# Block-causal attention then a gated two-layer network on one core: a planned kernel gets other planned load times, and a few of its operations move to other engines and places

## The chip, the cores and the metric

The program runs on one core of one Trainium2 chip. Its time is the device time of the whole program in microseconds (us), lower is better. The engines are named as the profile names them: PE (TensorE matmuls), PEld (its weight loads), DVE (VectorE), ACT (ScalarE), POOL (GpSimd) and SP (SyncE, which only issues transfers here). ACT and POOL issue transfers as well.

## The reference

Attention over 8 batches of 8 heads, 576 positions of 64 elements, masked by blocks of 64 positions; then two matrix products with an activation between them, over 4608 rows (8 batches x 576 positions) of 512 elements.

```python
scores = (1 / np.sqrt(64)) * q @ k.transpose(0, 1, 3, 2)
scores = np.where(pos[:, None] // 64 >= pos[None, :] // 64, scores, -1e9)
attn = softmax(scores); attn_out = attn @ v
x = attn_out.transpose(0, 2, 1, 3).reshape(4608, 512)
h = x @ w_in                       # 512 -> 2048
g = h * (1.0 / (1.0 + np.exp(-beta * h)))
out = g @ w_out                    # 2048 -> 512
```

q, k, v, w_in and w_out come as float32 and the result is float32. Inside, the kernel multiplies in bf16 and f16.

## The kernel before

The kernel writes no order of its own. It makes a list of operations (`P.op`), each with an engine, a planned duration, the operations that it depends on, the buffers that it takes and a priority `prio` (lower goes first). `Plan.schedule` plays them through in a model of the core and so fixes, once, the order in which each engine issues its instructions; `assign` then gives the semaphore waits. On the chip each engine goes through its own list in that order and waits where it must. For a transfer the plan takes `xfer` (ns) as the time that it holds its queue, and adds a fixed landing time. A changed `xfer` or `prio` therefore changes nothing but the order in which instructions stand on all the engines, as far as the plan runs differently.

**Attention** goes by units of two heads, a *pair*; batch 0 has pairs 0 to 3 (`u` = 0 to 3), batch 1 pairs 4 to 7. In batches 0 and 1 q and k of a pair come as two 256 KB loads (`ST`, L724, buffers ST0 to ST7 by turn, semaphores `s_d_S0_0` to `s_d_S7_0`: q of pair 0 is S0, k of pair 0 is S1, and so on; pair 4 takes S0 and S1 again). Each is cast to bf16 (L731, `QKn`; on POOL except for q of pairs 0 and 3, which DVE casts), turned by PE in four small matmuls (L742), and copied from PSUM to `QKT` by DVE (L752). The scores of a pair are three groups of matmuls in batch 0 (L837), each group with an exponential on ACT (L857, 128x1024 twice and 128x512) into `E`, and a mask: a memset of zeros over the forbidden corner (L865 and L867). `E` is multiplied by V (L912 in batch 0, L1051 later), then divided by the row sums on DVE (L930, L937; later L1063, L1070), turned again (L946) and copied into `xT` (L953), the input of the network. Pair 3's `E` lies in the buffer gT1. The last 64 rows of batch 0 are done apart, "late" (L975 to L1038), from loads of their own (semaphore `s_d_TR0_0`, cast at L692). V of batch 0 comes as 128 KB loads (`s_d_V0_0` to `s_d_V0_7`) and is cast by POOL to `Vn` (L575); V of batch 1 comes as four blocks and two tails (L598, L601) and is cast at L624. From batch 2 on, q and k come in 576 KB loads (L765), POOL casts them (L776) and a transposing transfer on SP turns them (L783).

**The network** goes by chunks of 512 rows, r = 0 to 8. A chunk has 16 FF1 blocks, j = 0 to 15: four 128x512 matmuls of `xT` by a column block of `w_in` (L1297), a tanh on ACT (L1307) and a product on DVE that writes `gT` (L1311). Block j needs part j // 4 of `w_in`. Chunk 0 then does FF2 plainly: 64 matmuls of 128x512 by `w_out` (L1333), sixteen of them for each of four parts of `w_out`. Later chunks use a scheme with fewer products (L1214) on sums that DVE makes (L1158, L1178). The four parts of `w_in` (L524, semaphores `s_d_win0` to 3) and of `w_out` (L529) are cast during their transfer and so are issued by POOL, between its casts. Where PE would stand idle early on, the plan puts fill matmuls on zeros (L548, L457).

What issues a part of the weights is set at the end: `WH()` names, for the four parts of `w_in`, the load whose landing they wait for, and

```python
        for w, o in zip(win, WH()):
            w.deps.append(o)
        for i, w in enumerate(wout):
            w.deps += ld["V", 1, 0] if i < 2 else [ld["K", 8]]
```

so that parts 1, 2 and 3 of `w_in` wait for k of pairs 4, 5 and 5, and parts 0 and 1 of `w_out` for all six loads of V of batch 1.

Of the kernel before, what the change touches and what calls it, by code (L numbers as in the profile page):

```python
# [359 lines left out]
def bass_blockwise_causal_attn__then__act_swish_beta_kernel(  # L360
# [10 lines left out]
    with es:  # L371
# [59 lines left out]
        P = Plan()  # L431
# [53 lines left out]
        for i in range(NQ):  # L485
# [5 lines left out]
            o = P.op("POOL", 120, mk(lambda g, i=i: g.memset(Vn[i][:, 4, :, 64:66], 0.0)), prio=-5)  # L491
# [6 lines left out]
        for i in range(NQ, NE + 1):  # L498
# [10 lines left out]
                  xfer=100, dma=("d_beta", 1), prio=3.45)  # L509
# [3 lines left out]
                  deps=[bt, c2], tiles=[tb], lat=400, mode="full", prio=9)  # L513
# [6 lines left out]
        win, wout = [], []  # L520
# [39 lines left out]
        load, ld, early = {}, {}, []  # L560
        VC = -38.5
        tl = {}
        for b in range(B):
# [27 lines left out]
            for h0, h1, e, tt in PARTS[b]:  # L591

                vs = []
                for i in tt:
# [10 lines left out]
                    if e == "SP":  # L605
                        o = P.op("SP", 300 + 550 * n, fv, tiles=[ts], xfer=1400 * n,
                                 prio=3.5 + 0.1 * (h0 > 0) if b == 0 else 4 * b + (3.5 if b < 2 else 0.5),
                                 dma=["d_V", h0, 1])
                    else:
                        o = P.op("POOL", 150 + 1450 * n, fv, tiles=[t], xfer=1400 * n, prio=-30 if b == 0 else 4 * b + (3.5 if b < 2 else 0.5), dma=["d_VP", h0, 1])  # L610
                        o.after = lastv if b else None
# [36 lines left out]
        def WH():  # L648
            return ld["V", 0, 1], ld["K", 4], ld["K", 5], ld["K", 5]

        xt, spare = [], []
        HALF, LP, VP = (3,), .2, 200 + 2
        copied, more0 = [], []
        early6, rows = [], []
        QKI, QKX = 550, 2700
        for u in range(NU):
            b, c = divmod(u, NPAIR)
# [9 lines left out]
            if b < QB:  # L667

                if c == 0:
# [10 lines left out]
                    for w, src in enumerate((q, k)):  # L680
# [4 lines left out]

                        o = P.op("SP", 650, fl, tiles=[te_], xfer=900, prio=u + 0.5 if b else 3.8, dma=["d_TR", 0, 1])
                        o.pkt = 48.0
# [31 lines left out]
                for w, (nm, src) in enumerate((("Q", q), ("K", k))):  # L719
# [6 lines left out]

                    o = ld[nm, u] = P.op("SP", 540, fl, tiles=[ts], xfer=(760, 950)[b], prio=u, dma=["d_S", 0, 1])
                    o.pkt = 48.0
# [122 lines left out]
            for g0 in range(4 if b else 3):  # L851
                o, ps = qk[g0]
                if g0 < 3:
# [9 lines left out]
                    def fz(g, e, g0=g0, te=te, two=two, off3=off3):  # L863
# [3 lines left out]
                        return g.memset(bass.AP(a.tensor, a.offset, [a.ap[0], [512, 2], [off3, 2], [1, 64]]), 0.0)  # L867
                    zs.append(P.op("DVE" if b or g0 == 2 else "POOL", 160 if g0 != two else 220, fz, deps=[x], tiles=[te], prio=-20 if b or g0 == 2 else -37))
                else:
# [252 lines left out]
        for i, w in enumerate(wout):  # L1122
            w.deps += ld["V", 1, 0] if i < 2 else [ld["K", 8]]

# [302 lines left out]
```

## Time and profile before

| | us |
|---|---|
| time, median of 3 runs | 330.4 (327.89 to 335.31) |
| the profiled execution's time | 329.3 |
| its span, first to last instruction | 327.5 |
| PE busy | 316.4 (97% of the span) |
| DVE busy | 219.9 (67%) |
| ACT busy | 211.8 (65%) |
| POOL busy | 84.5 (26%) |
| mean granted TensorE clock | 0.999 |

The time is 1.8 us longer than the span in the profiled execution: that is what lies around the instructions. Busy time of PE is a union of the matmuls' recorded stretches. Matmuls overlap (one of 128x512 is recorded with 379 ns, while eight of them in a row take 1.73 us), so short waits between them do not show as idle time.

### The profile page before, as it was taken

The page shows a single profiled execution, that of the slowest core. Times are in us where ns is not written, and L with a number is a line of the kernel's source. Part 1 is how long each engine was busy: PE and PEld are TensorE (multiplying, and loading weights), DVE is VectorE, ACT ScalarE, POOL GpSimd, SP SyncE. Part 2 cuts the span into 40 slices and gives each one's busy share as a digit, 9 for nine tenths or more (in the row PEclk, how much of TensorE's full clock was granted, in tenths as well). Part 3 has the DMA queues.
Part 4 walks back from the last instruction along what each step waited for, and adds up shares of the span by engine and source line. Part 5 has one row for each costly group of instructions (what it writes and reads, how often), then busy time and mean ns, then how long its engine had stood idle before and what let it go on. Part 6 is the DMA issues. An engine that isn't in the chain of part 4 may idle for free.

```text
span 327.5 us, 7435 instructions
## 1 busy us (share of the span) xinstructions
PE 316.4 (97%) x3101; PEld 200.3 (61%) x3012; DVE 219.9 (67%) x455; ACT 211.8 (65%) x312; POOL 84.5 (26%) x137
## 2 busy tenths in 40 slices
PE   7698999999999999999999999999999999999996
PEld 2454446445786457854776467666666766666695
DVE  5657857578763789368843996659576866666742
ACT  2769891388557886499657866885978454544521
POOL 4768090073073046103520541150000000000000
PEclk9999999999999999999999999999999999999999
DMA  7999999999999999997999999999030310111023
GB/s 224 225 302 233 215 211 199 169 292 189 226 252 221 222 193 218 186 240 152 196 190 241 231 197 195 199 169 152 0 74 2 104 34 32 62 36 35 6 92 128
DMA packets 156706, 53.58 MB, mean 164 GB/s; under 512 B 139120, under 2 KB 156160, under 8 KB 156672
## 3 DMA queue, kind: packets, MB, share of 16 engines
q1 hardware_dynamic: 144112, 40.46, 65.8%
q10 hardware_dynamic: 8336, 8.46, 8.2%
q0 software_dynamic: 4224, 4.19, 7.8%
q8 instruction: 24, 0.39, 0.5%
q14 instruction: 10, 0.08, 0.1%
HBM read 36.71 MB, written 9.44 MB: 141 GB/s over the span
## 4 chain that ended last, share of the span: by engine, by line
PE 83%; DMA 5%; DVE 4%; ACT 4%; issue 2%; SPq 1%; POOL 1%; POOLq 0%
PE PS L1297 34%; PE PS L1214 29%; PE PS L1051 8%; PE PS L837 6%; PE PS L1333 4%; DMA w_in<-in_moe_w_in_dram 3%; ACT E L857 2%; DMA ST<-in_q_dram 2%; DVE gT L1311 1%; ACT th L1307 1%; DVE QKT L752 1%; SPq L724 1%; DMA xT<-xq 1%; PE PS L1099 1%; PE PS L912 0%
## 5 line engine op out<-in xcount | busy, mean ns | idle before, releaser
L1297 PE MATMUL PS<-xT,w_in 128*128 128x512 bf16 x576 | 137.7, 379 | 3.1 <-DMA w_in<-in_moe_w_in_dram 1.2
L1307 ACT ACTIVATE th<-PS,beta 128x512 f32<-128x512 f32 x144 | 97.0, 701 | 54.9 <-PE PS L1297 53.9
L1311 DVE SCALAR_TENSOR_TENSOR gT<-th,PS 128x512 f16<-128x512 f32 x144 | 95.2, 681 | 35.8 <-ACT th L1307 35.4
L857 ACT ACTIVATE E<-PS 128x1024 bf16<-128x1024 f32 (+1 forms) x90 | 87.5, 1014 | 22.4 <-PE PS L837 21.5
L1297 PEld LDWEIGHTS PS<-xT,w_in 128*128 128x128 bf16 x576 | 53.1, 98 | 58.5 <-issue 2.2
L1214 PE MATMUL PS<-w_out,gT 128*128 128x256 f16 x512 | 63.0, 273 | 0.1
L1214 PEld LDWEIGHTS PS<-w_out,gT 128*128 128x128 f16 x512 | 49.0, 98 | 12.1 <-issue 0.8
L776 POOL CAST QKn<-ST 128x640 bf16<-128x640 f32 x48 | 37.0, 771 | 24.9 <-DMA ST<-in_k_dram 13.9
L624 POOL CAST Vn<-Vs 128x640 bf16<-128x640 f32 x24 | 19.6, 815 | 91.7 <-DMA Vs<-in_v_dram 90.6
L1236 ACT ACTIVATE ost<-PS 128x512 f32<-128x512 f32 x32 | 19.3, 604 | 28.5 <-PE PS L1214 28.5
L1214 PE MATMUL PS<-OV 128*128 128x256 f16 (+1 forms) x264 | 31.8, 270 | 0.0
L1051 PEld LDWEIGHTS PS<-Vn,E 128*128 128x128 bf16 x810 | 27.5, 97 | 3.9 <-issue 0.4
L837 PE MATMUL PS<-QKT 64*128 64x448 bf16 (+7 forms) x292 | 28.6, 295 | 0.5 <-ACT E L857 0.5
L1051 PE MATMUL PS<-Vn,E 128*128 128x65 bf16 x810 | 28.4, 193 | 0.0
L1214 PEld LDWEIGHTS PS<-OV 128*128 128x128 f16 x264 | 24.5, 98 | 6.1 <-issue 0.6
L1178 DVE TENSOR_TENSOR OV<-gT 128x1024 f16<-128x1024 f16 x32 | 23.9, 753 | 0.6
L837 PEld LDWEIGHTS PS<-QKT 64*128 64x128 bf16 (+1 forms) x292 | 13.3, 94 | 17.7 <-issue 3.6
L1070 DVE TENSOR_TENSOR xq<-PS,inv 128x640 bf16<-128x640 f32 x28 | 23.0, 820 | 0.5
L1239 DVE SCALAR_TENSOR_TENSOR ost<-PS,ost 128x512 f32<-128x512 f32 x22 | 15.2, 689 | 9.5 <-PE PS L1214 6.9
L865 DVE MEMSET E<- 64x64 uint32 x57 | 6.3, 112 | 17.9 <-ACT E L857 16.0
L1214 PE MATMUL PS<-OV,gT 128*128 128x256 f16 (+1 forms) x136 | 16.0, 266 | 0.0
L1333 PE MATMUL PS<-w_out,gT 128*128 128x512 f16 x64 | 15.3, 379 | 0.0
(106 smaller groups left out, 189.9 us busy)
## 6 DMA issues: line engine op xcount, KB each, us to landing
out_dram<-ost ACTq DMA_DIRECT2D x32, 256.0 KB, 3.9
ST<-in_q_dram SPq DMA_DIRECT2D x12, 576.0 KB, 6.2
ST<-in_k_dram SPq DMA_DIRECT2D x12, 576.0 KB, 7.2
Vs<-in_v_dram SPq DMA_DIRECT2D x24, 256.0 KB, 4.6
ST<-in_q_dram SPq DMA_DIRECT2D x8, 256.0 KB, 5.9
ST<-in_k_dram SPq DMA_DIRECT2D x8, 256.0 KB, 6.1
w_in<-in_moe_w_in_dram POOLq DMA_DIRECT2D x4, 512.0 KB, 8.4
w_out<-in_moe_w_out_dram POOLq DMA_DIRECT2D x4, 512.0 KB, 8.9
```

The lines of the kernel that those rows point to most:

```text
L624: return g.tensor_copy(Vn[t.slot][:, 0:n, g0:g1, 0:64], Vs[ts.slot][:, 0:n, g0:g1, :])
L776: return g.tensor_copy(QKn[tn.slot][:].rearrange("p a w n -> p (a w n)")[:, 640 * (2 * a + w):][:, 0:640] .rearrange("p (t h d) -> p t h d ...
L837: z = g.matmul(o, QKT[tqk.slot][r, uu % 2, 1, k0:k0 + m], x)
L857: return g.activation(E3[es_(te)][:, g0, :, 0:n], PS[:, ps.slot:ps.slot + 2, 0:n], ACT.Exp, scale=0.125)
L1051: z = g.matmul(o, eblk(te, t, i, h), Vn[Tv.slot][:, t, 2 * c + h, 0:65], start=(t == 0), stop=(t == i))
L1070: return g.tensor_tensor(xq[xq_(tx)][:].rearrange("p i (h d) -> p h i d", h=2), both(pv, 0, 64), x, ALU.mult)
L1178: return P.op("DVE", dve_t(SZ * HC / 2), mk(lambda g: g.tensor_tensor(fo(), fx(), fy(), op)), deps=deps, tiles=tiles, prio=prio)
L1214: x = g.matmul(PS[:, pw.slot, HM * w + c0:HM * w + c1], fa()[:, j, 128 * w:128 * w + 128], fb()[:, j, c0:c1], start=first and (pair or w = ...
L1297: z = g.matmul(PS[:, ph.slot, :], w_in[:, c, 128 * j:128 * j + 128], xT[:, c, row % RX:row % RX + RC], start=(c == 0), stop=(c == 3))
L1307: return g.activation(th[tt.slot][:], PS[:, ph.slot, :], ACT.Tanh, scale=beta[:, j:j + 1])
L1311: return g.scalar_tensor_tensor(out=gT[tg.slot][:, j, :], in0=th[tt.slot][:], scalar=1.0, in1=PS[:, ph.slot, :], op0=ALU.add, op1=ALU.mult)
L1333: z = g.matmul(PS[:, po.slot, 0:d1 - d0], gT[tg.slot][:, j, 128 * w:128 * w + 128], w_out[:, j, d0:d1], start=(j == 0), stop=(j == NJ - 1))
```

## The change

Five edits:

1. The loads of q and k of pairs 0 to 3 get planned queue times of their own, `EARLYX`, instead of 760 ns each; those of batch 0's late rows get 1100 ns instead of 900.
2. The masks of pair 3 are made by DVE instead of POOL (the condition `u == 3`).
3. Part 1 of `w_in` waits for the loads of the late rows (`ld["T", 0]`) instead of k of pair 4; part 2 for k of pair 4 instead of pair 5.
4. Parts 0 and 1 of `w_out` wait for part 3 of `w_in` and for V's second and fourth block of batch 1, instead of all six loads of V.
5. For that, V's blocks of batch 1 get semaphores of their own: blocks 0 and 1 share one (`s_d_V1_9`), blocks 2 and 3 another (`s_d_V1_10`); the tails keep `s_d_V1_0`. A priority expression for b == 0, a case that does not occur there, goes.

```diff
-                                 prio=3.5 + 0.1 * (h0 > 0) if b == 0 else 4 * b + (3.5 if b < 2 else 0.5),
-                                 dma=["d_V", h0, 1])
+                                 prio=4 * b + (3.5 if b < 2 else 0.5),
+                                 dma=["d_V", 9 + i // 2 if b == 1 and i < 4 else h0, 1])
...
-            return ld["V", 0, 1], ld["K", 4], ld["K", 5], ld["K", 5]
+            return ld["V", 0, 1], ld["T", 0][1], ld["K", 4], ld["K", 5]
...
+        EARLYX = (650, 750, 1950, 900, 850, 800, 850, 900)
...
-                        o = P.op("SP", 650, fl, tiles=[te_], xfer=900, prio=u + 0.5 if b else 3.8, dma=["d_TR", 0, 1])
+                        o = P.op("SP", 650, fl, tiles=[te_], xfer=900 if b else 1100, prio=u + 0.5 if b else 3.8, dma=["d_TR", 0, 1])
...
-                    o = ld[nm, u] = P.op("SP", 540, fl, tiles=[ts], xfer=(760, 950)[b], prio=u, dma=["d_S", 0, 1])
+                    o = ld[nm, u] = P.op("SP", 540, fl, tiles=[ts], xfer=EARLYX[2 * u + w] if u < 4 else 950, prio=u, dma=["d_S", 0, 1])
...
-                    zs.append(P.op("DVE" if b or g0 == 2 else "POOL", 160 if g0 != two else 220, fz, deps=[x], tiles=[te], prio=-20 if b or g0 == 2 else -37))
+                    zs.append(P.op("DVE" if b or g0 == 2 or u == 3 else "POOL", 160 if g0 != two else 220, fz, deps=[x], tiles=[te], prio=-20 if b or g0 == 2 or u == 3 else -37))
...
-            w.deps += ld["V", 1, 0] if i < 2 else [ld["K", 8]]
+            w.deps += [win[3], ld["V", 1, 0][1 + 2 * i]] if i < 2 else [ld["K", 8]]
```

From L655 on, a line has a number higher by one in the changed kernel (L752 is L753 there, L1297 is L1298).

Through the plan these edits move instructions on every engine. Three places matter below.

On DVE at the start of the program, before (QKT0 holds pairs 0 and 1, QKT1 pairs 2 and 3; S6 is the load of q of pair 3):

```order
L731 CAST QKn0<-ST0 128x512 [waits s_d_S0_0]
L752 COPY QKT0<-PS 128x512 [waits s_PE] x3
L731 CAST QKn1<-ST1 128x512 [waits s_d_S6_0]
L752 COPY QKT0<-PS 128x512 [waits s_PE]
L752 COPY QKT1<-PS 128x512 [waits s_PE] x2
L865 MEMSET E0 64x2x32 [waits s_ACT]
L752 COPY QKT1<-PS 128x512 [waits s_PE] x2
```

and now:

```order
L753 COPY QKT0<-PS 128x512 [waits s_PE] x4
L753 COPY QKT1<-PS 128x512 [waits s_PE]
L866 MEMSET E0 64x2x32 [waits s_ACT]
L753 COPY QKT1<-PS 128x512 [waits s_PE]
L732 CAST QKn1<-ST1 128x512 [waits s_d_S6_0]
L753 COPY QKT1<-PS 128x512 [waits s_PE] x2
```

The cast of q of pair 3 stood behind three copies and now stands behind six. A little later on DVE, in the changed kernel, from pair 2's last mask (E2) over pair 1's division (inv1, xq1) to pair 3's last mask:

```order
L866 MEMSET E2 64x2x32 [waits s_ACT]
L866 MEMSET gT1 64x2x32 [waits s_ACT]
L931 RECIPROCAL inv1<-PS 128x8 [waits s_PE]
L954 COPY xT<-PS 128x512 [waits s_PE]
L938 TENSOR_TENSOR xq1<-PS,inv1 128x2x4x64 [waits s_DVE]
L868 MEMSET gT1 64x2x2x32 [waits s_ACT]
L866 MEMSET gT1 64x2x32 [waits s_ACT]
```

Of the three masks of pair 3 (gT1) only the last was on DVE before.

On POOL, from the last cast of V of batch 0 to the second part of `w_in`, before:

```order
L575 CAST Vn0<-Vs0 128x4x2x64 [waits s_d_V0_6,s_d_V0_7,s_POOL]
L867 MEMSET E2 64x2x2x64 [waits s_POOL,s_ACT]
L692 CAST QKt<-gT1 128x512 [waits s_POOL,s_d_TR0_0]
L865 MEMSET gT1 64x2x64 [waits s_ACT,s_POOL]
L867 MEMSET gT1 64x2x2x64 [waits s_POOL,s_ACT]
L731 CAST QKn0<-ST0 128x512 [waits s_POOL,s_d_S0_0]
L524 DMA w_in<-in_moe_w_in_dram 128x4x512 [waits s_d_S1_0]
```

and now:

```order
L575 CAST Vn0<-Vs0 128x4x2x64 [waits s_d_V0_6,s_d_V0_7,s_POOL]
L524 DMA w_in<-in_moe_w_in_dram 128x4x512 [waits s_d_TR0_0]
L693 CAST QKt<-gT1 128x512 [waits s_POOL]
L732 CAST QKn0<-ST0 128x512 [waits s_POOL,s_d_S0_0]
L524 DMA w_in<-in_moe_w_in_dram 128x4x512 [waits s_d_S1_0]
L732 CAST QKn0<-ST0 128x512 [waits s_POOL]
```

Part 1 of `w_in` moved ahead of the late rows' cast and of k of pair 4, part 2 took its place, and the masks of gT1 left POOL.

On PE, from the end of pair 4's first scores (L837 on QKT2, which holds pairs 4 and 5) over the fourth FF1 block of chunk 0 to the fifth, which waits for part 1 of `w_in`, before:

```order
L837 MATMUL PS<-QKT2 128x448 x2
L742 MATMUL PS<-identB,QKn0 128x128 [waits s_POOL,s_ACT]
L742 MATMUL PS<-identB,QKn0 128x128 x3
L1297 MATMUL PS<-xT,w_in 128x512 [waits s_DVE]
L1297 MATMUL PS<-xT,w_in 128x512 x3
L837 MATMUL PS<-QKT2 128x320 [waits s_DVE,s_ACT]
L837 MATMUL PS<-QKT2 128x320
L837 MATMUL PS<-QKT2 128x192 x2
L837 MATMUL PS<-QKT2 64x64 x2
L742 MATMUL PS<-identB,QKn0 128x128 [waits s_DVE,s_POOL]
L742 MATMUL PS<-identB,QKn0 128x128 x3
L1297 MATMUL PS<-xT,w_in 128x512 [waits s_DVE,s_d_win1]
```

and now, from the fifth block to the first scores of pair 4 (Vn0 by gT1 is the late rows' product with V, OV their counterpart of batch 1):

```order
L1298 MATMUL PS<-xT,w_in 128x512 [waits s_d_win1,s_ACT]
L1298 MATMUL PS<-xT,w_in 128x512 x3
L1008 MATMUL PS<-Vn0,gT1 128x65 [waits s_POOL]
L1008 MATMUL PS<-Vn0,gT1 128x65 x39
L1298 MATMUL PS<-xT,w_in 128x512 [waits s_DVE]
L1298 MATMUL PS<-xT,w_in 128x512 x3
L698 MATMUL PS<-identB,OV 128x128 [waits s_POOL,s_DVE]
L698 MATMUL PS<-identB,OV 128x128 x3
L1298 MATMUL PS<-xT,w_in 128x512 x4
L838 MATMUL PS<-QKT2 128x512 [waits s_DVE]
```

The scores of pair 4 stood between the third and the fourth FF1 block and ahead of the fifth; now seven FF1 blocks stand ahead of them.

## The prediction

> **What bounds the kernel.** I read the page's busy times first, then the span cut into stretches, to see where PE has time that is not work.
>
> ```profile
> PE 316.4 (97%) x3101; PEld 200.3 (61%) x3012; DVE 219.9 (67%) x455; ACT 211.8 (65%) x312; POOL 84.5 (26%) x137
> ```
> ```profile
> core 0: us, PE busy (x) PEld busy (x) DVE busy (x) ACT busy (x) POOL busy (x), PEclk, DMA share, GB/s
> 0.00:22.80 22.80, 17.99 (x217) 8.85 (x185) 13.85 (x40) 12.36 (x17) 13.49 (x36) 1.00 0.99 243
> 22.80:31.10 8.30, 7.12 (x87) 3.57 (x84) 5.85 (x16) 7.54 (x11) 7.18 (x20) 1.00 1.20 263
> 31.10:52.50 21.40, 20.66 (x274) 12.05 (x268) 15.11 (x38) 16.38 (x26) 10.12 (x15) 1.00 1.18 211
> ...
> 60.00:310.00 250.00, 248.25 (x2338) 159.15 (x2289) 175.44 (x343) 171.14 (x254) 53.66 (x68) 1.00 0.78 152
> 310.00:327.50 17.50, 14.89 (x149) 12.96 (x146) 6.44 (x14) 3.67 (x6) 0.00 (x0) 0.98 0.32 106
> ```
>
> PE is the bound, and at full clock. From 60 to 310 us it idles 1.75 us of 250, from 310 on 2.61 us, which is the drain of the last product and its stores. Whatever the change does after 60 us, it cannot win more than those 1.75. So the question is the first 60 us: when the first FF1 block can start, and what holes follow. In the chain that ended last that stretch reads so:
>
> ```profile
> 10.06 1.80 DVE QKT L752 x3
> ...
> 21.47 9.49 DMA w_in<-in_moe_w_in_dram
> 31.00 1.04 PE PS L1297 x4
> 32.04 1.21 PE PS L1007 x40
> ...
> 114.50 2.59 PE PS L1297 x12
> ```
>
> The bound is not PE at two places here: DVE's copies at 10 us, and part 1 of `w_in`, issued at 21.47 and landed 9.49 us later, for which PE waits at 31. The last row gives the price of an FF1 block where nothing waits: 2.59 / 3 = 0.86 us.
>
> ```profile
> 7.25 0.72 PE L837 MATMUL PS<-QKT 64*128 64x512 bf16 x8
> ...
> 11.04 0.61 PE L837 MATMUL PS<-QKT 64*128 64x512 bf16 x6
> ...
> 22.82 1.03 PE L1297 MATMUL PS<-xT,w_in 128*128 128x512 bf16 x4
> ...
> 25.14 1.04 PE L1297 MATMUL PS<-xT,w_in 128*128 128x512 bf16 x4
> ...
> 31.00 1.04 PE L1297 MATMUL PS<-xT,w_in 128*128 128x512 bf16 x4 [1.18 <-DMA w_in<-in_moe_w_in_dram]
> ...
> 52.53 1.89 PE L1333 MATMUL PS<-w_out,gT 128*128 128x512 f16 x8
> ```
>
> The first FF1 block starts at 22.82. Behind it both programs hold the same matmuls (I counted them from the order: 576 of FF1, 64 and 912 of FF2, 280 of scores and so on), so the time moves by the shift of this start, plus the change in PE's holes behind it. Everything is reckoned against the profiled execution: 329.3 us, of which 327.5 span and 1.8 around it. The median of the runs, 330.4, is 1.1 above it, and the runs spread over 7.4 us.
>
> **Start: planned loads and masks (edits 1 and 2).** DVE first, then ACT and POOL:
>
> ```profile
> 7.13 0.69 DVE L752 COPY QKT<-PS 128x512 bf16<-128x512 bf16 x1 [0.87 <-PE PS L742]
> 9.63 0.43 DVE L731 CAST QKn<-ST 128x512 bf16<-128x512 f32 x1 [1.81 <-DMA ST<-in_q_dram]
> 9.98 1.88 DVE L752 COPY QKT<-PS 128x512 bf16<-128x512 bf16 x3
> ...
> 19.10 0.11 DVE L865 MEMSET gT<- 64x64 uint32 x1 [1.10 <-ACT gT L857]
> ```
> ```profile
> 7.68 2.43 ACT L857 ACTIVATE E<-PS 128x1024 bf16<-128x1024 f32 x3 [5.44 <-PE PS L837]
> 11.48 4.26 ACT L857 ACTIVATE E<-PS 128x1024 bf16<-128x1024 f32 x5 [1.37 <-PE PS L837]
> ...
> 16.61 2.43 ACT L857 ACTIVATE gT<-PS 128x1024 bf16<-128x1024 f32 x3
> ...
> 27.89 1.93 ACT L857 ACTIVATE E<-PS 128x1024 bf16<-128x1024 f32 x2
> ```
> ```profile
> 7.15 0.62 POOL L731 CAST QKn<-ST 128x512 bf16<-128x512 f32 x1 [0.51 <-DMA ST<-in_k_dram]
> ...
> 8.92 0.62 POOL L731 CAST QKn<-ST 128x512 bf16<-128x512 f32 x1 [0.15 <-DMA ST<-in_k_dram]
> ...
> 18.33 0.62 POOL L692 CAST QKt<-gT 128x512 bf16<-128x512 f32 x1 [1.33 <-DMA gT<-in_k_dram]
> ...
> 21.47 0.74 POOL L524 DMA_DIRECT2D w_in<-in_moe_w_in_dram  x1 [1.09 <-DMA ST<-in_k_dram]
> ...
> 40.57 0.74 POOL L529 DMA_DIRECT2D w_out<-in_moe_w_out_dram  x1 [7.74 <-DMA OV<-in_v_dram]
> ```
>
> Before, DVE stood 1.81 us at the cast of pair 3's q while k of pair 1, cast since 7.77, could not be copied: scores of pair 1 at 11.04, ACT idle 1.37. Now three copies go ahead of that cast. Pair 1's k: cast done 7.77, turned, copied by about 9.1. PE then turns k of pair 2 (cast done 9.54) and scores pair 1 at about 10.0, exponential 0.43 later as in the rows (7.25 to 7.68). A pair's three exponentials take 2.43, so pairs 1 to 3 end ACT at 10.4 + 3 x 2.43 = 17.7, against 16.61 + 2.43 = 19.04. Nothing later holds ACT: pair 3's k and q reach QKT at about 13, as before, needed at 15.3. The first scores also lose the transpose ahead of them, but ACT then only waits longer for pair 1. From the last exponential to the first FF1 block DVE's and PE's chain took 22.82 - 19.10 = 3.7 us. I keep it, since its members are the same, and add 0.1 for a division that now stands behind a mask. Start at 21.5: **-1.3 us**. Ends: -1.9 (ACT never idle after a first exponential at 6.8: 6.8 + 9.7 = 16.5, and the chain 0.6 longer), and 0 (DVE's masks hold the division of pair 1, so the chain grows by all that ACT won).
>
> **Part 1 of `w_in` (edit 3).** It now waits for the late rows' k, landed at 18.3 (end of POOL's wait above), so it goes out at 18.3 instead of 21.47; behind it the late rows' cast is 0.74 later, needed by PE only at about 21. Landing takes, over the four parts:
>
> ```profile
> DMA to landing us min/median/max: 6.4/8.4/10.0
> ```
>
> That gives 24.7 to 28.3, likeliest 26.7. PE reaches the fifth block at 21.5 + 2.3 (22.82 to 25.14: the first block, the late scores and the turn of pair 4's k, all of which still stand ahead) + 3 x 0.86 = 26.4. So the wait of 1.18 falls to about 0.3: **-0.9 us**, between -1.2 and +0.5 (landing at 28.3).
>
> ```profile
> gT<-in_q_dram SPq DMA_DIRECT2D x1, 128.0 KB, 3.5
> gT<-in_k_dram SPq DMA_DIRECT2D x1, 128.0 KB, 5.6
> ```
>
> These two equal loads went out 0.7 us apart, the second while part 0 of `w_in` had just started: it took 2.1 us longer. So an earlier part 1 may delay what SP has under way, k of pair 4 first; that is the second rival below. The Trainium skill, DMA: Bandwidth & Descriptors, section "Issuing engines are not separate DMA queues", says that transfers of all issuing engines run on the same 16 DMA engines and interleave, and that issuing from several saves the issue time alone. By that rule the landing is moved and not won, and the sum is that rival's, 328.8, instead of 328.1. The two rows agree with it in direction.
>
> **What now stands ahead of pair 4's scores.** Seven FF1 blocks and the late product: scores at 26.7 + 3 x 0.86 + 1.21 + 0.2 = 30.7, exponential at 31.1 instead of 27.89, 3.2 us later. ACT's work from there:
>
> ```profile
> L1307 ACT ACTIVATE th<-PS,beta 128x512 f32<-128x512 f32 x15 | 10.3, 740 | 2.0 <-PE PS L1297 2.0
> L857 ACT ACTIVATE E<-PS 128x1024 bf16<-128x1024 f32 x9 | 9.0, 1038 | 1.6 <-PE PS L837 1.6
> L857 ACT ACTIVATE gT<-PS 128x1024 bf16<-128x1024 f32 x3 | 3.2, 1138 | 0.0
> ```
>
> (groups of ACT from 27 to 52 us.) Twelve exponentials at 0.97 (1.93 / 2) and nine remaining tanh at 0.7, with four small tails, are about 18.5 us, so until 49.6 if ACT never waits. PE has FF1 blocks 7 to 15, scores, transposes and two products with V before FF2: the 21.4 us of the stretch from 31.1 to 52.5 less three FF1 blocks (2.6) and the late product (1.2), 17.6, until 48.3. The order is fixed and gives ACT no lead. From 31.1 to 52.5 ACT idled 5.0 of 21.4 us before; 3.2 of these are gone, and some of PE's waits will show. Nothing to all of 3.2 us; I take **+1.0**, a third, since the 0.74 us that PE idled in that stretch is the nearest row.
>
> **`w_out` and V (edits 4 and 5).** POOL stood 7.74 us for all of V before it issued part 0, which was used at 52.53. Now part 0 goes out when part 3 of `w_in` has landed (issued near 28, plus 8.4), part 1 when V's fourth block has, before the 40.5 that all six took: between some 36 and 39 us, in time already spent waiting; V's casts wait for the tails as before, at 40.5, with one issue of 0.74 fewer ahead. Parts 2 and 3 still wait for k of batch 2. FF2 is reached at 48.3 and PE's waits, about 50, and its first half, 32 x 0.216 = 6.9 us (1.73 for 8), with V's products stands before part 2 is wanted, near 60.
>
> ```profile
> DMA to landing us min/median/max: 7.7/8.9/12.1
> ```
>
> With these landings, part 1 is there by 51 at worst and part 2, issued at 47, by 59. **0**; without the cover up to +1.
>
> **From 60 us on.** The same matmuls in another order on all queues. On SP the first transposing transfer of batch 2 moves behind V's two tails and one 576 KB load:
>
> ```profile
> 49.56 12.33 SPq L783 DMA_TRANSPOSE QKT<-QKn  x1
> ```
>
> Its issue ended at 61.9. PE now finishes FF2 of chunk 0 (64 x 0.216 = 13.8) and three FF1 blocks (2.6) before it wants the result, and has products with V and transposes among them: not before 50 + 16.4 + 2 = 68. **0**, between -1 (of the 1.75 us of idle) and +3.
>
> Sum: -1.3 - 0.9 + 1.0 = -1.2, so 328.1 on the profiled execution's scale, and 329.2 on the median's. I forecast 328.6 us, between the two.
>
> **Rivals.**
>
> *The start doesn't move.* DVE's two new masks wait for ACT with pair 1's division behind them, and DVE is in the chain's last 3.7 us. For it: the two masks stand ahead of a division and a copy to xT. Against: that division ends near 17.6, when pair 3's exponentials end. The change then does not do at the start what its planned times say: the 1.3 goes, the wait for `w_in` (PE there at 27.7) falls by 1.2, and the 1.0 stays: 329.1.
>
> *The hole moves from `w_in` to k of pair 4.* PE must turn it ahead of the third FF1 block. It landed at 21.4 (end of POOL's 1.09 wait). Delayed by 2.1 us (the two equal loads above) to 3.1 (as much as part 1 goes out earlier), it lands at 23.5 to 24.5, POOL then issues part 2 (0.74) and casts (0.62): 24.9 to 25.9, where PE arrives at 24.4. A hole of 0.5 to 1.5, 1.0 taken, and none for `w_in` behind it: 329.3 - 1.3 - 1.2 + 1.0 + 1.0 = 328.8.
>
> *Slower: ACT becomes the bound before FF2.* If `w_in` lands at 28.3, pair 4's first exponential is at 32.7, ACT's 18.5 us end at 51.2, and the 3.6 us of waits that its groups show (2.0 + 1.6) come on top: 54.8, against 50 for PE. PE's two products with V and the last blocks hang on it: +4.8 instead of +1.0 with -1.3 and +0.5: 333.3. It decides from the point where pair 4's first exponential passes about 32.
>
> *Late transposes.* One 576 KB load of q takes, from issue to landing:
>
> ```profile
> ST<-in_q_dram SPq DMA_DIRECT2D x12, 576.0 KB, 6.2
> ```
>
> If the load costs the transfer all of its 6.2 us, the issue ends at 68.1, just when PE wants the result, which still has to land. With V's two tails ahead as well I price it in the upper half of the term's range, +2.3: 330.4. It decides from a delay of some 5 us on. Against it: two parts of `w_out` are out of the way earlier.
>
> **Chances.** Forecast 0.52, start unmoved 0.14, moved hole 0.13, ACT the bound 0.12, late transposes 0.05, and more won than summed (start -1.9, holes gone, 325) 0.04. The range of 8 in 10 is 325.2 to 333.3: the terms' lower ends, -1.9 - 1.2 - 1 from 329.3, and the slower rival. A measurement here tells some 2%, 6.6 us, from no change; faster by that needs 324 and slower 337; only run-to-run spread on top of the extreme cases reaches either, 0.04 each.
>
> **What would show it.** Right: first FF1 block near 21.5, ACT's second group of exponentials near 10.4 with little idle before it, no 1.81 us at DVE's cast, PE's wait for `w_in` under 0.5. Wrong: first FF1 block still at 22.8; a wait of PE for POOL's cast at 24; PE idle over 2.5 us between 31 and 52; a hole near 70 put down to QKT's transfer.

## The result, and the profile after

The changed kernel takes 334.7 us (median; 333.9 to 334.9) where the kernel before takes 329.9 beside it: 1.0155 of it, 95% interval 1.0119 to 1.0191, so slower by 1.5%. Run again in another session it was 1.0216 (1.0177 to 1.0256). Executions that took over 1.5% longer than the fastest of the same kernel (one of the first session, 367.7 us at a granted clock of 0.853) are left out of the ranges and ratios, and so is the trace of run e2. The forecast was 328.6 with a range to 333.3.

The profiled execution takes 333.9 us, its span 332.1, against 329.3 and 327.5. The page's busy times and the stretches, cut at the same places as those of the prediction:

```profile
PE 319.6 (96%) x3120; PEld 201.1 (61%) x3015; DVE 220.7 (66%) x456; ACT 210.4 (63%) x313; POOL 84.3 (25%) x135
```
```profile
0.00:22.80 22.80, 20.06 (x262) 9.58 (x218) 14.24 (x42) 13.71 (x19) 13.23 (x35) 1.00 1.01 247
22.80:31.10 8.30, 6.10 (x73) 3.71 (x74) 4.13 (x6) 4.83 (x8) 7.15 (x19) 0.90 1.19 244
31.10:52.50 21.40, 20.82 (x203) 10.40 (x192) 15.39 (x38) 16.29 (x25) 7.53 (x11) 0.96 1.05 197
60.00:310.00 250.00, 245.66 (x2341) 157.05 (x2290) 172.82 (x340) 167.19 (x250) 53.96 (x68) 1.00 0.80 154
```

Two rows are worse: from 22.8 to 31.1 us PE is busy 6.10 us instead of 7.12, and from 60 to 310 it idles 4.34 us instead of 1.75. The granted clock is below 1 in the second and third rows, which it was in neither of them before. The start went as forecast. DVE, then ACT and PE (idle before a row and what ended it in brackets):

```profile
9.72 0.69 DVE L753 COPY QKT<-PS 128x512 bf16<-128x512 bf16 x1
10.32 0.58 DVE L732 CAST QKn<-ST 128x512 bf16<-128x512 f32 x1
```
```profile
9.89 4.75 ACT L858 ACTIVATE E<-PS 128x1024 bf16<-128x1024 f32 x6 [0.61 <-PE PS L838]
...
34.92 1.93 ACT L858 ACTIVATE E<-PS 128x1024 bf16<-128x1024 f32 x2
```
```profile
21.25 1.03 PE L1298 MATMUL PS<-xT,w_in 128*128 128x512 bf16 x4
...
28.52 1.02 PE L1298 MATMUL PS<-xT,w_in 128*128 128x512 bf16 x4 [2.20 <-DMA w_in<-in_moe_w_in_dram]
29.38 2.32 PE L1008 MATMUL PS<-Vn,gT 128*128 128x65 bf16 x40
...
51.34 1.03 PE L1334 MATMUL PS<-w_out,gT 128*128 128x512 f16 x4
...
208.36 1.04 PE L1298 MATMUL PS<-xT,w_in 128*128 128x512 bf16 x4 [2.56 <-DMA xT<-xq]
```

DVE no longer waits at the cast, ACT's second group starts at 9.89, the first FF1 block at 21.25 (22.82 before). But PE waits 2.20 us for part 1 of `w_in` at the fifth block, not 0.3; the late product behind it takes 2.32 us instead of 1.21 at half clock; pair 4's first exponential is at 34.92, where 31.1 was forecast and 27.89 stood before; and there is a wait of 2.56 us for `xT` at 208. That last wait lies in the stretch that the prediction had put at nothing. GpSimd shows a second thing that it had put at nothing:

```profile
37.71 0.74 POOL L529 DMA_DIRECT2D w_out<-in_moe_w_out_dram  x1 [4.58 <-DMA OV<-in_v_dram]
39.40 0.74 POOL L529 DMA_DIRECT2D w_out<-in_moe_w_out_dram  x1 [0.95 <-DMA OV<-in_v_dram]
...
48.96 1.51 POOL L777 CAST QKn<-ST 128x640 bf16<-128x640 f32 x2 [5.74 <-DMA ST<-in_q_dram]
52.03 1.48 POOL L529 DMA_DIRECT2D w_out<-in_moe_w_out_dram  x2 [1.56 <-DMA ST<-in_k_dram]
```

`w_out` goes out early, as planned, and now the cast of q of batch 2 waits 5.74 us for its load. The two loads of q and k of batch 2 (issued between 35 and 40.5 us), before and after:

```profile
DMA to landing us min/median/max: 7.1/7.4/7.6
```
```profile
DMA to landing us min/median/max: 11.0/11.8/12.7
```

### The profile page after: what moved, and what is told of

The parts are those of the page before. It is cut to its first block, busy times and chain, and to the rows that moved or that the text cites. A ratio compares the mean times of both kernels' runs of the same rounds, so it can differ in the third digit from the quotient of the medians.

```text
span 332.1 us, 7458 instructions
## 1 busy us (share of the span) xinstructions
PE 319.6 (96%) x3120; PEld 201.1 (61%) x3015; DVE 220.7 (66%) x456; ACT 210.4 (63%) x313; POOL 84.3 (25%) x135
## 4 chain that ended last, share of the span: by engine, by line
PE 80%; DMA 6%; ACT 4%; DVE 3%; SPq 3%; issue 2%; ACTq 0%
PE PS L1298 33%; PE PS L1215 28%; PE PS L1052 7%; PE PS L838 5%; PE PS L1334 4%; DMA w_in<-in_moe_w_in_dram 3%; ACT E L858 2%; DMA gT<-in_k_dram 2%; SPq L570 2%; DVE gT L1312 2%; ACT th L1308 2%; SPq L725 1%; DMA xT<-xq 1%; DVE OV L753 1%; PE PS L1100 1%
## 5 line engine op out<-in xcount | busy, mean ns | idle before, releaser
L1298 PE MATMUL PS<-xT,w_in 128*128 128x512 bf16 x576 | 137.7, 381 | 6.4 <-DMA xT<-xq 2.6
L1298 PEld LDWEIGHTS PS<-xT,w_in 128*128 128x128 bf16 x576 | 53.1, 98 | 63.2 <-issue 6.1
L838 PE MATMUL PS<-QKT 64*128 64x448 bf16 (+8 forms) x292 | 28.3, 295 | 0.4 <-DVE QKT L753 0.2
L1052 PE MATMUL PS<-Vn,E 128*128 128x65 bf16 x810 | 27.7, 193 | 0.0
L1071 DVE TENSOR_TENSOR xq<-PS,inv 128x640 bf16<-128x640 f32 x28 | 22.8, 819 | 0.4
L1179 DVE TENSOR_TENSOR OV<-gT 128x1024 f16<-128x1024 f16 x32 | 22.4, 707 | 1.0 <-PE PS L1215 0.4
L1334 PE MATMUL PS<-w_out,gT 128*128 128x512 f16 x64 | 14.6, 379 | 0.0
```

Source lines behind the costliest of these rows:

```text
L838: z = g.matmul(o, QKT[tqk.slot][r, uu % 2, 1, k0:k0 + m], x)
L1052: z = g.matmul(o, eblk(te, t, i, h), Vn[Tv.slot][:, t, 2 * c + h, 0:65], start=(t == 0), stop=(t == i))
L1071: return g.tensor_tensor(xq[xq_(tx)][:].rearrange("p i (h d) -> p h i d", h=2), both(pv, 0, 64), x, ALU.mult)
L1179: return P.op("DVE", dve_t(SZ * HC / 2), mk(lambda g: g.tensor_tensor(fo(), fx(), fy(), op)), deps=deps, tiles=tiles, prio=prio)
L1298: z = g.matmul(PS[:, ph.slot, :], w_in[:, c, 128 * j:128 * j + 128], xT[:, c, row % RX:row % RX + RC], start=(c == 0), stop=(c == 3))
L1334: z = g.matmul(PS[:, po.slot, 0:d1 - d0], gT[tg.slot][:, j, 128 * w:128 * w + 128], w_out[:, j, d0:d1], start=(j == 0), stop=(j == NJ - 1))
```

## The experiments

All were timed in five rounds beside the kernel before. The table gives each ratio with its interval, and how much later than in the kernel before (profiled executions) ACT starts the tanh of five FF1 blocks: the first and last of chunk 0, the last of chunks 3 and 4, and the end of the span. Where the order differs, a block stands behind other work of PE; the columns between the first and the end are therefore compared among kernels with the same order behind the head: the old rest (before, e4, f2, f4, g1, g2, h1 to h3) or the new one (changed, f1, e1, e3, f3).

```
                                     ratio [95%]              first  c0 end  c3 end  c4 end   end
changed                              1.0155 [1.012, 1.019]    -1.57   -0.50    2.59    2.56   4.60
f1 changed, again                    1.0216 [1.018, 1.026]    -1.23   -2.27    4.80    3.47   7.92
e1 product ahead of block 5          1.0210 [1.016, 1.026]    -1.15   -2.94    4.62    7.33   6.91
e2 w_out's old waits                 1.0108 [1.007, 1.015]    -       -       -       -       -
e3 xT ahead on SP at 200 us          1.0132 [1.010, 1.017]    -0.26    1.05    4.64    3.84   3.14
e4 edits 1, 2 alone                  1.0042 [1.001, 1.007]    -0.47    0.68    0.38    0.41   0.50
f2 new head, old rest                1.0163 [1.014, 1.019]    -1.00    4.83    5.19    4.50   4.48
f3 old head, new rest                1.0097 [1.005, 1.014]     0.23   -1.95    2.16    2.94   4.13
f4 f2 with product ahead             1.0195 [1.017, 1.022]    -1.05    5.39    5.79    5.10   4.99
g1 e4's order, new waits             1.0184 [1.013, 1.024]    -0.59    0.96    1.19    6.08   6.69
g2 f2's order, old waits             1.0236 [1.018, 1.029]    -1.66   10.46   10.69   10.00   9.89
g3 edit 3 alone                      1.0070 [1.004, 1.010]     0.93   -0.92    2.30    3.05   3.14
g4 changed without edit 3            1.0167 [1.012, 1.021]    -0.72    0.26    1.66    5.08   6.89
h1 e4's order, edit 4                1.0191 [1.016, 1.022]    -1.11   -0.08   -0.32    4.53   4.71
h2 e4's order, edit 3                1.0079 [1.005, 1.011]     0.47    2.07    2.08    1.40   1.29
h3 e4's order, w_out behind k        1.0090 [1.006, 1.012]    -1.91   -0.20    0.72    0.04   0.31
```

**First: is the loss early, late, or in one edit?** *e1*, one number of the planner:

```
-            win.append(P.op("POOL", 1000, fwi, xfer=3150, ...
+            win.append(P.op("POOL", 1000, fwi, xfer=5300 if a == 1 else 3150, ...
```


> The changed kernel, with one number more: the planner is told that part 1 of w_in takes 5300 ns of transfer instead of 3150. From 28 to 50 us this puts the late product (40 matmuls) and three fills ahead of the fifth FF1 block; up to there and from the first FF2 block on the order is that of the changed kernel. Theory A (the early loss counts: PE waits 2.2 us for w_in, then runs at half clock for 3.4 us, and both last to the end): the late product covers 1.2 us of the wait, the clock stays whole, and 2 to 2.5 us are won: about 332.4 (331.5 to 333). Theory B (what is lost before 60 us is given back before 110, only the holes behind 130 us count): same as the changed kernel, 334.2 to 334.9. Profile: under A no drop of the granted clock near 29.5 us.

1.0210, no gain. Chunk 0 ends 2.4 us ahead of the changed kernel, but the end comes 2.3 us behind it. A wait at the first blocks of chunk 1 (2.45 us at 71, for a copy of DVE to `xT`) and one of 2.5 us for `xT` at 171 take all of it. So theory A's gain did not come. That the hole near 29 us is harmless doesn't follow, since another wait took its place.

*e2* puts back one line:

```
-            w.deps += [win[3], ld["V", 1, 0][1 + 2 * i]] if i < 2 else [ld["K", 8]]
+            w.deps += ld["V", 1, 0] if i < 2 else [ld["K", 8]]
```


> The changed kernel with the waits of w_out's first two parts as before (all six transfers of V's second batch) and all else changed. Its order is that of the changed kernel up to the first FF2 block at 51 us, and another one behind it. Theory A (early loss): the wait for w_in and the half clock stay, so at most 1 us is won: 333.5 to 335. Theory B (the holes behind 130 us are SP's order as it fell out of a new plan): another late order, with another loss there; in before these holes cost 3.7 us less, so about 331 (330 to 333), and the holes of 2.6 us near 206 and 1.3 us near 166 gone. If edit 4 itself does harm by sending w_out at 37.7 to 39.4 us, the time falls too, but then the difference is to be seen between 37 and 60 us.

1.0108: part of the loss goes with edit 4, though the order behind 51 us changes too, so the run can't tell which of the two it was.

*e3* moves one transfer behind two others on SP, after the plan:

```
         P.schedule()
+        sp = P.order["SP"]
+        t1 = sp.pop(111)
+        sp.insert(113, t1)
+        t1.start = sp[112].start + 1
```


> The changed kernel, its plan untouched but for one place: on SP, at 199.7 us, the transposing transfer of k and q of one batch (4.5 us of issue) goes behind the two transposing transfers of xT instead of ahead of them. Theory B: xT lands about 2 us earlier, PE's hole of 2.56 us at 206 shrinks to about 0.6, and 2 us are won to the end: 332.7 (332 to 333.2). Rival: the turned k and q land 2.5 to 4 us later and their scores wait instead, or the store and V loads behind: 334.2 to 334.9.

1.0132, in the direction of theory B. In the first fence SP and PE as changed, in the second with the two `xT` ahead:

```profile
199.71 4.51 SPq L784 DMA_TRANSPOSE QKT<-QKn  x1
204.26 2.61 SPq L1088 DMA_TRANSPOSE xT<-xq  x2
```
```profile
200.58 2.85 SPq L1088 DMA_TRANSPOSE xT<-xq  x2
203.47 4.42 SPq L784 DMA_TRANSPOSE QKT<-QKn  x1
...
207.13 0.81 PE L1298 MATMUL PS<-xT,w_in 128*128 128x512 bf16 x3
```

The wait of 2.56 us is gone: PE reaches the block 1.2 us ahead of the changed kernel, although it was 2.05 us behind it at chunk 3's end. What is left of e3's loss stands early: PE waits until 30.19 us for `w_in`, for 2.56 us, and the granted clock is at half from 29.9 to 33.3; at 71 it waits another 0.71.

*e4* takes the kernel before and adds edits 1 and 2 (the `EARLYX` row, `xfer=1100`, and `or u == 3` in the two conditions of the masks).

> The kernel before with edits 1 and 2 alone (planned landings of the first loads, masks of the fourth pair on VectorE); w_in, w_out and V as before. Theory A: the first FF1 block near 21.3 us instead of 22.8, w_in part 1 still issued near 21.5 and waited for by about 1 us more than before unless the plan puts other work there; the gain of 1.5 us is kept or halved: 328.4 to 329.5. Theory B (any new plan costs holes behind 130 us of some 3 us by chance, whatever edit makes it): 330 to 333, with the loss behind 130 us.

1.0042. Its order joins that of the kernel before again behind 72 us of the plan, and its times stay within 0.6 us of it from the second chunk on. So the start edits, with their 1.3 us at the start, win nothing that lasts; they cost 0.1 to 0.7%. Some 0.45 us of that lie outside of the span: time less span is 2.26 us in e4 and 1.8 before.

**Second: head or rest?** The planner gets a list of operations for each engine, and takes nothing else but the fills (in g1, g2 and h1 to h3 the fills are in the list too):

```
-                        if e not in o.engs:
+                        if e not in o.engs or self.force and not o.fill and o.idx != self.force[e][sum(not x.fill for x in order[e])]:
...
+        P.force = {e: list(map(int, x.split())) for e, x in ORDER.items()}
         P.schedule()
```

> The changed kernel unaltered, beside the three below. Every theory: 1.012 to 1.019 of the kernel before. What is open is what repeats: the first FF1 block at 21.25 us was seen once, and two kernels with the same order up to there had it at 22.6 to 22.8; if the start's gain is not firm it comes out between 21.2 and 22.8 here. The wait for w_in near 29 us should be 1.9 to 2.6 us again, the holes at 166 to 174 and 206 us together some 3 to 4 us.

> The changed kernel's order on every engine for what the planner places in the first 45 us (all five edits are in it), and behind that the order of the kernel before: each engine takes its operations from a written list. Theory B (the loss is the late order): 0.998 to 1.004 of before, and chunk by chunk the time lies within 1 us of before from the second chunk on. Theory A (the loss is early: the wait for w_in, half clock, pair 4 late): 1.007 to 1.015. Each half of it would give about 1.008.

> The reverse: none of the edits, the order of the kernel before in the first 45 us, then that of the changed kernel. Theory B: as slow as the changed kernel, 1.011 to 1.018, with holes ahead of FF1 blocks between 160 and 210 us that wait for xT. Theory A: 0.997 to 1.004.

> The second kernel of this call with one thing more: the late product stands ahead of the fifth FF1 block, as in the run that told the planner 5300 ns for part 1 of w_in. That one ended chunk 0's FF1 2.4 us ahead of the changed kernel and 2.9 ahead of before. Theory B, with that lead kept behind the old order: 0.990 to 0.998 of before, the fastest of all. Rival: the lead is spent before chunk 1, as it was there (the rest waits for something else, transposes and V's products of the second batch): 0.998 to 1.005.

Neither theory alone: the new head costs 1.6% with the old rest (f2), the new rest 1.0% with the old head (f3). f3 holds none of the five edits, only the order behind 45 us, and k of batch 2 lands at 44.9 us in it, as before (44.6). Yet PE waits 4.1 us for `xT`, the second time at the block of the changed kernel's 2.56:

```profile
168.43 1.67 PE L1297 MATMUL PS<-xT,w_in 128*128 128x512 bf16 x7 [2.16 <-DMA xT<-xq]
...
208.13 0.81 PE L1297 MATMUL PS<-xT,w_in 128*128 128x512 bf16 x3 [1.96 <-DMA xT<-xq]
```

So most of that wait comes of the new order alone. The pair of `xT` transfers went out at 203.22 in f3 and at 204.26 in the changed kernel, so the rest of the edits add 1.0 us there. e3 shows what it is in the order: the transposing transfer of q and k ahead of the pair.

f1 came out above the 1.019 that every theory allowed. Its wait at that block is 3.86 us, and it has another that the first execution did not have:

```profile
63.32 1.29 DVE L1159 TENSOR_TENSOR OV<-w_out 128x1024 f16<-128x1024 f16 x2 [3.12 <-DMA w_out<-in_moe_w_out_dram]
...
69.81 4.22 PE L1298 MATMUL PS<-xT,w_in 128*128 128x512 bf16 x11 [2.50 <-DVE xT L1110]
```

DVE's copy to `xT` stands behind six sums over `w_out`, and the sums wait for its late parts: parts 2 and 3 go out at 52.2 us here and at 52.0 in the first execution (46.5 before), since they wait for k of batch 2. In the first execution the copy starts at 68.20 and PE comes to it at 68.8, late by its hole at 29 and the half clock; in f1, where the wait for `w_in` is 1.69 us and the clock stays whole, PE comes at 67.3 and waits. e1's wait at 71 is the same one (DVE waits 2.89 us there). In f3 the sums don't wait.

In f2 all is lost by the end of chunk 0. Its stretches, behind them those of e4, which differs from it in the order of the head and in edits 3 to 5:

```profile
46.00:52.50 6.50, 3.34 (x52) 1.76 (x48) 1.34 (x7) 5.58 (x9) 1.44 (x2) 1.00 1.07 207
```
```profile
46.00:52.50 6.50, 6.45 (x121) 4.84 (x121) 5.06 (x14) 4.41 (x7) 4.49 (x7) 1.00 1.18 202
```

PE is busy 3.34 us of 6.50, ACT 5.58. PE waits for ACT:

```profile
49.71 0.39 PE L838 MATMUL PS<-OV 64*128 64x512 bf16 x2 [2.04 <-ACT E L858]
...
51.44 1.99 PE L1052 MATMUL PS<-Vn,E 128*128 128x65 bf16 x60 [1.12 <-ACT gT L858]
```
```profile
35.31 1.93 ACT L858 ACTIVATE E<-PS 128x1024 bf16<-128x1024 f32 x2
...
50.36 1.94 ACT L858 ACTIVATE gT<-PS 128x1024 bf16<-128x1024 f32 x2 [0.71 <-PE PS L838]
```

The second batch's exponentials run from 35.31 to 52.30. That is the rival "ACT becomes the bound before FF2", with first exponential and place as it said (past 32; before FF2) and a price of 3.2 us (the waits of 2.04 and 1.12). f4, forecast at 0.990 to 1.005, missed by far: its sixth to thirteenth blocks of chunk 0 are 1 to 8 us ahead of f2's, and it ends the chunk 0.6 us behind f2. It too waits for ACT, four times for 0.8 to 1.3 us, but its granted clock is also at half from 47.2 to 54.0 us, so how much of that end is ACT's isn't shown.

**Third: order or waits?** g1 keeps e4's order on PE, ACT, DVE and SP and takes GpSimd's order and all waits from the changed kernel; g2 is the reverse with f2's order.

> All five edits, but TensorE, ScalarE, VectorE and SyncE keep from start to end the order that edits 1 and 2 alone give (pair 4's scores behind the third FF1 block, the old rest); only GpSimd's order and waits are the changed kernel's, so part 1 of w_in goes out near 19 us, part 2 near 22, w_out's first parts near 38 to 40. Theory C (the head's loss is the order of compute: pair 4's exponentials stand behind seven FF1 blocks, ACT ends the second batch 4.4 us later): as edits 1 and 2 alone, or better by the wait for w_in: 0.996 to 1.006 of before. Theory D (the transfers: parts 1 and 2 of w_in, issued earlier, hold up k and q of pairs 6 and 7 by 2.5 to 4.6 us, and PE waits for those): 1.010 to 1.018.

> The reverse: edits 1 and 2 alone with their order on GpSimd (part 1 of w_in near 22 us, part 2 near 28), but TensorE, ScalarE, VectorE and SyncE in the order that had the changed kernel's head and the old rest. Theory C: as slow as that one or slower, 1.014 to 1.025, since the fifth FF1 block now waits for w_in until about 31 us and pair 4's exponentials stand behind it. Theory D: 1.000 to 1.007.

Both are slow, so neither theory alone holds here either. g2 shows the order's: the fifth block waits 4.3 us for `w_in`, pair 4 stands behind it, chunk 0 ends 10.5 us late. g1 shows another: chunk 0 ends 1 us late and chunk 3 as well, and then one wait makes all the rest. Theory D named the wrong place for it (pairs 6 and 7).

```profile
171.55 1.67 PE L1298 MATMUL PS<-xT,w_in 128*128 128x512 bf16 x7 [0.87 <-DMA xT<-xq]
```
```profile
175.55 2.64 PE L1298 MATMUL PS<-xT,w_in 128*128 128x512 bf16 x7 [3.93 <-DMA xT<-xq]
```

(the first block of chunk 4, in e4 and in g1.) Two runs without a list, edit 3 alone on the kernel before and edit 3 taken out of the changed one:

```
-            return ld["V", 0, 1], ld["K", 4], ld["K", 5], ld["K", 5]
+            return ld["V", 0, 1], ld["T", 0][1], ld["K", 4], ld["K", 5]
```


> The kernel before with edit 3 alone (w_in's parts issued earlier). The plan that follows also puts seven FF1 blocks and the late product ahead of pair 4's scores, and another rest. Theory C: 1.008 to 1.020, pair 4's first exponential past 32 us. If edit 3 needs edits 1 and 2 to do harm (which bring the first FF1 block forward): 0.996 to 1.004.

> The changed kernel without edit 3. The plan that follows has pair 4's scores behind the third FF1 block again, so no loss in the head under theories C and D; its rest is a new one (edit 4), differing from before's until 264 us: 1.003 to 1.011, with chunk 0 ending within 1 us of before. If edits 1, 2 or 4 make the loss: 1.013 to 1.022.

Edit 3 alone costs 0.7%: theory C forecast 0.8 to 2.0 and pair 4's first exponential past 32; it came at 31.75, just at the point from which the rival decides. Without it the changed kernel keeps its loss (1.0167), with a head on time (+0.26) and 6.2 us of waits for `xT`.

**Fourth: which transfer?** In e4's order on every engine but GpSimd, h1 adds edit 4 (`w_out` part 1 also ahead of V's casts), h2 edit 3, and h3 makes all of `w_out` wait for k of batch 2:

```
h3:
-            w.deps += ld["V", 1, 0] if i < 2 else [ld["K", 8]]
+            w.deps += [ld["K", 8]]
```


> Edits 1, 2, 4 and 5 in the order that edits 1 and 2 alone give on every engine, but for GpSimd, where w_out's part 1 goes out ahead of V's casts. Theory E (w_out's 2 MB ahead of q and k of batch 2 put SyncE's stream back, and it has no slack until PE meets it at 172 us): k of batch 2 lands near 50 us or later instead of 45.7, the stream is 2 to 3 us later at 100 to 160 us, PE waits 2.5 to 4 us for xT near 172: 1.010 to 1.018 of before. Rival (it is w_in's earlier parts): 1.002 to 1.007, as edits 1 and 2 alone.

> Edits 1, 2, 3 and 5 in that same order; GpSimd's order is the changed kernel's, but w_out waits for all of V as before. Theory E: k of batch 2 near 46 us, the stream at 100 to 160 us within 1 us of that of edits 1 and 2 alone, no wait over 1.5 us at 172: 1.000 to 1.007. Rival: 1.010 to 1.018. The wait of PE for w_in part 1, which its order puts at the fifth block near 32 us, should be gone in both readings.

> Edits 1 and 2 in their own order, with one wait changed the other way: all four parts of w_out wait for k of batch 2. Theory E: k of batch 2 lands 2 to 3 us earlier than 45.7, the stream is 1 to 2 us earlier at 100 to 160 us, the wait of 0.9 us at 172 goes, 0.995 to 1.002 of before if w_out still lands in time. Price of the other side: part 0 goes out near 43.5 instead of 41.7, part 1 near 45.5, so FF2, which wants them at 52 to 55, may wait up to 2 us, and V's casts stand behind part 0 on GpSimd: then 1.004 to 1.010.

Theory E holds for h1 and h2 in kind; both lie just above its ranges (1.0191 against 1.018, 1.0079 against 1.007). What h2 loses stands at the end of chunk 0 already (2.07 us). In h1 `w_out` goes out at 39.54 and 40.83 (e4: 41.67 and 45.43), and k of batch 2 takes 13.0 us to land instead of 7.4:

```profile
39.54 0.74 POOL L529 DMA_DIRECT2D w_out<-in_moe_w_out_dram  x1 [6.24 <-DMA w_in<-in_moe_w_in_dram]
40.83 0.74 POOL L529 DMA_DIRECT2D w_out<-in_moe_w_out_dram  x1 [0.54 <-DMA OV<-in_v_dram]
...
51.41 1.48 POOL L529 DMA_DIRECT2D w_out<-in_moe_w_out_dram  x2 [5.14 <-DMA ST<-in_k_dram]
```
```profile
DMA to landing us min/median/max: 5.9/9.5/13.0
```
```profile
DMA to landing us min/median/max: 7.2/7.3/7.4
```

(the loads of q and k in h1, then in e4.) SP issues in the same order in e4, h1, h2 and h3, one transfer behind the other, so a lag can be followed. h1 against e4 is 1.9 us late at the first transposing transfer of batch 2 (54.42 us, 0.9 of it a wait for the cast of k), 1.2 at 63 us, 0.5 at 130, and 2.6 at the pair below. So it changes on its way. In h2 k lands 3.9 us later than in e4 (49.6, not near 46 as theory E had it), and no lag follows: V's loads hold SP until 53.0 us there, and the cast of k is done by 52.9 (h1: 54.4). The pair of `xT` transfers for chunk 4 goes out, in e4, h1, h2 and h3:

```profile
167.64 2.54 SPq L1088 DMA_TRANSPOSE xT<-xq  x2
```
```profile
170.21 2.55 SPq L1088 DMA_TRANSPOSE xT<-xq  x2
```
```profile
167.68 2.63 SPq L1088 DMA_TRANSPOSE xT<-xq  x2
```
```profile
166.16 2.58 SPq L1088 DMA_TRANSPOSE xT<-xq  x2
```

and PE in h1 stands, while in h2 and h3 it has no wait there at all:

```profile
174.35 3.00 PE L1298 MATMUL PS<-xT,w_in 128*128 128x512 bf16 x7 [4.37 <-DMA xT<-xq]
```

PE in h1 was 0.32 us ahead of the kernel before at chunk 3's end, and is 4.53 behind at chunk 4's. The pair is 2.6 us later in h1 than in e4. h3 has it 1.5 us earlier than e4, as theory E said, and no wait, but its other half failed: nothing is won (1.0090). Its profiled execution, the fastest of its six, ends 0.31 us behind; what takes the lead away isn't shown. No version beat the kernel before.

## Why the prediction was wrong, step by step

*Start, -1.3: right.* The row shows -1.57. Over the thirteen profiled executions with edits 1 and 2 in the table, the first tanh is 1.91 us earlier to 0.47 later than the one of the kernel before, 0.9 earlier on average; in the three without the edits (before, f3, g3) 0.4 later on average. So -1.3 again, though one execution could have shown anything in those 2.4 us. What fails is that it was carried to the end: h1 and h3, 1.11 and 1.91 us ahead at the first block, are 0.08 and 0.20 ahead at the last of chunk 0.

*Part 1 of `w_in`, -0.9: wrong.* The chain of the changed kernel (start, length) has it

```profile
18.74 9.65 DMA w_in<-in_moe_w_in_dram
```

so it landed at 28.4, at the late end of the 6.4 to 10.0 that I had quoted. PE came to the block at 26.3 (28.52 less 2.20), as forecast (26.4). The wait became 2.20 instead of 1.18, so +1.0, outside of the bounds of -1.2 to +0.5. The upper bound was wrong by its own terms: 28.3 less 26.4 is a wait of 1.9, which is +0.7. The half clock behind it, 3.41 us long and by that an estimated 1.7 us dear, was not foreseen. Both together make +2.7 of the -0.9, the largest miss of the profiled execution; f1 waited 1.69 us and kept its clock.

*Pair 4 behind seven blocks, +1.0: mis-sized, both ways.* Pair 4's first exponential came at 34.9, past the 32 from which my slower rival was to decide, and the rival's condition, the landing at 28.3, came about to 0.1 us. But in the changed kernel its price did not come: from 31.1 to 52.5 us PE idles 0.58 us (0.74 before) and spends some 0.45 on fills. FF2 starts at 51.34 there, and the last two exponentials of the batch are left to 56.4. With the old rest (f2) PE waits 3.2 us for ACT. That f2 ends chunk 0 at +4.83, the rival's +4.8, is chance: its start (-1.0), its wait of 2.01 us for `w_in` and the half clock behind that are in it too.

*`w_out`, 0: wrong.* I asked when the parts would land, and not what they push aside. With two parts (2 MB of f32 in all) ahead, k of batch 2 lands 5.4 us later (h1 against e4); in the changed kernel it lands 7.2 us later than before, of which 2.1 are a later issue. With e4's order that costs 4.2 us (h1 against e4 at the end). In the changed kernel's own order it sends parts 2 and 3 out 5.5 us later, and f1 and e1 wait 2.5 us at 70 us for what hangs on them. The rule of the Trainium skill, DMA: Bandwidth & Descriptors, section "Issuing engines are not separate DMA queues", that transfers of all issuing engines interleave on the same 16 DMA engines, I had weighed for `w_in` alone; it applied here, and h1 agrees with it: GpSimd's transfers 2.1 and 4.6 us earlier, SP's load 5.4 us later.

*From 60 us on, 0: wrong.* The same matmuls in another order were taken to cost nothing, without a look at when SP would send each `xT`. f3 shows that the new order alone loses: two waits of 2.16 and 1.96 us, and 4.13 us at the end. 1.75 us of PE idle were read as a cap on gains, which they are, but not as a sign of how little slack there is. The kernel before already met the stream: its first block of chunk 4 waited 0.61 us for `xT`.

```profile
170.92 1.90 PE L1297 MATMUL PS<-xT,w_in 128*128 128x512 bf16 x8 [0.61 <-DMA xT<-xq]
```

PE and SP's stream arrive there together, so a lag of the stream shows: 2.6 us of it made h1's wait 3.5 us longer than e4's. I looked for late transposes at 70 us (0.05). What showed there were the copies to `xT`, and the late stream showed at 168 to 211.

The causes do not add: in f2 PE is some 5 us late by the end of chunk 0, and the same late k then costs nothing more. How the changed kernel's own loss divides can be estimated from the matmuls of its trace. I count the columns that they have streamed, without the fills, and those on 64 rows by half (eight of 512 columns take 0.72 us, eight on 128 rows 1.89). By that count its profiled execution is 1.6 us ahead of the one before at 22 us, 1.8 behind from 60 to 72, 2.1 behind at 200, and 4.7 at 213. So 1.8 of the 4.6 us were lost early, where -1.2 was forecast, and 2.6 at the wait at 208. f1 lost at 70 and at 211 instead, so the shares change from one execution to the next. Taking edit 4 out leaves 1.0108, edit 3 out 1.0167, both 1.0042, each with another order. That e4 itself is slower than before is at the edge of what was measured.

## What to carry to other kernels

A bound engine that is busy 99% says how much can be won, not how much can be lost: search its few short waits for a second stream that runs just as full, and ask of every transfer that is moved forward which other transfer it delays and when that one's stream next meets the bound engine. Where a new plan reorders a queue that runs full, its order is a change of its own, to be priced even if no transfer is added (f3). Where a plan moves other work (here FF1 blocks) ahead of what starts another engine's long chain (the exponentials), add up that engine's chain from its new start to its consumer in the order that follows: with the old rest it cost 3.2 us of waits, with the new one hardly anything.

## What the hardware showed

The clock: after waits of PE of 2.20 us (changed kernel, granted clock of a stretch in the last but two columns), 4.37 (h1), 2.01 (f2) and others between them the granted clock fell to half for 3.41 us (6.83 in g2). In the profiled execution of before, whose longest wait behind the first FF1 block was 1.18 us, it did so only in its last 0.6 us.

```profile
29.50:33.00 3.50, 3.50 (x45) 2.60 (x43) 1.57 (x3) 0.69 (x1) 2.53 (x5) 0.52 1.24 228
```
```profile
174.00:177.50 3.50, 3.15 (x10) 1.42 (x12) 0.69 (x1) 0.80 (x2) 0.00 (x0) 0.57 1.02 191
```

The Trainium skill, TensorE: Matmul & The Clock Gate, section "HAM oscillation — how this bites in real kernels", says not to leave PE idle for more than about 3.4 us. The length of the drop agrees with that figure; the gaps that set it off were shorter in most of these runs (2.0 to 2.6 us). The length of a wait does not decide alone: the clock stayed whole after 3.33 us in g4, 2.45 in e1 (at 71 us) and 2.16 in f3, and in f4 it fell for 6.83 us although no wait in the 7.2 us ahead was longer than 1.12 (by its records PE idled 2.46 of them in all). What else decides isn't shown. A drop makes a wait dearer than its row: h1's wait is 3.76 us longer than that of the kernel before at that block, and h1 loses 4.85 us from the end of chunk 3 to that of chunk 4. It did not decide this case: of the first session's executions of the changed kernel, two had a mean clock of 1.000 (334.4 and 334.5 us) and three of 0.990 to 0.995 (333.9 to 334.9).
